# A Fourier-mixing and MLP kernel: the last chunk's output sent from SP and Scalar only, none from GpSimd

## Chip, cores, metric

The kernel runs on one core of a Trainium2 chip. The metric is the device time of one execution in microseconds (us), taken as the median of several.

## The reference

```python
batch, seq, dim = (8, 3008, 256);  d_ff = 2048

X = np.fft.fft(x, axis=1)
X = np.fft.fft(X, axis=2)
x = X.real.astype(np.float32).reshape(batch * seq, dim)

h = x @ w_in
g = h * np.clip(h + 3.0, 0.0, 6.0) / 6.0
out = g @ w_out                     # (24064, 256), float32
```

## The kernel before

The kernel works through four pairs of batches, twelve chunks to a pair. For each chunk TensorE computes both layers; the second layer's seven products are accumulated in PSUM, scaled by ScalarE, added up by GpSimd and transposed in 32 x 32 blocks by VectorE. SP sends the result to HBM. GpSimd also issues the loads: 16 pieces of the weights, 36 direct loads of `x` and 32 gathers.

The last chunk is different, since nothing follows to hide its end. VectorE does its additions (`finish_final`), and its two halves are sent by three engines in turn:

```python
def finish_final(ch):
    ...
    add(rn[:, 0, 0], e[:, 0], e[:, 1], nc.vector)
    turn(ch, os[0], 0, 0)
    ...
    turn(ch, os[0], 0, 1)
    send(ch, os[0], 0)                      # first half
    add_product(wn[:, 1], 4, wn[:, 0])
    for h in range(2):
        add(rn[:, 1, h], wn[:, 1], e[:, 2 + h], nc.vector)
        turn(ch, os[1], 1, h)               # the last transpose ends here
    send(ch, os[1], 1)                      # second half

def send(ch, o, m):
    queues = [nc.sync, nc.scalar, nc.gpsimd] if ch.final else [nc.sync]
    i = 0
    sl = 0
    while sl < ch.ns:
        b, k1 = ch.rows[m][sl]
        nb = 2 if sl + 1 < ch.ns and ch.rows[m][sl + 1] == (b + 1, k1) else 1
        for qd in range(DB):                # DB = 4
            queues[i % len(queues)].dma_start(
                out=out_k[ch.pr.p, k1, qd][:, 2 * b:2 * (b + nb)],
                in_=o[qd * DH:(qd + 1) * DH, 2 * sl:2 * (sl + nb)].rearrange(...))
            i += 1
        sl += nb
```

A half of the last chunk is eight sends, four of 32 KB and four of 16 KB. The loads that matter to the experiments are these:

```python
def load_forward(pr, c):
    ...
    nc.gpsimd.dma_start(out=xt[0:nr, 0:n, :], in_=rows[:, c * XC + 1:c * XC + 1 + n, :])
    if n < XC:
        nc.gpsimd.dma_start(out=xt[0:nr, n:XC, :], in_=rows[:, 0:1, :])
```

Of the kernel before, what the change touches and what calls it, by code (L numbers as in the profile page):

```python
# [56 lines left out]
def kernel(  # L57
# [10 lines left out]
    nc = tc.nc  # L68
# [338 lines left out]
    def finish_final(ch):  # L407
        n = ch.n
        e = ch.e[:, :, 0:n]
        w = epool.tile([P, 3, TB], F32, tag="w", bufs=1, name="w")  # L410
        ch.r = epool.tile([P, 2, 2, TB], F32, tag="r", name="r")
        wn, rn = w[:, :, 0:n], ch.r[:, :, :, 0:n]
        os = [epool.tile([P, TB // DH, 2, DH], F32, tag="o", name="o") for m in range(2)]

        def add_product(out, i, in1, sign=1.0):
            nc.vector.scalar_tensor_tensor(out, ch.acc[i // 2][:, i % 2, 0:n], sign / WS, in1,
                                           op0=AL.mult, op1=AL.add)

        add(rn[:, 0, 0], e[:, 0], e[:, 1], nc.vector)
        turn(ch, os[0], 0, 0)  # L420
        add_product(wn[:, 0], 5, e[:, 0], -1.0)
        add(wn[:, 2], wn[:, 0], e[:, 3], nc.vector)
        add_product(rn[:, 0, 1], 6, wn[:, 2])
        turn(ch, os[0], 0, 1)
        send(ch, os[0], 0)
# [3 lines that stand above are left out]
            turn(ch, os[1], 1, h)  # L429
        send(ch, os[1], 1)  # L430

    def store(ch, m):
        o = epool.tile([P, TB // DH, 2, DH], F32, tag="o", name="o")
        for h in range(2):
            turn(ch, o, m, h)
        send(ch, o, m)
# [4 lines left out]

    def send(ch, o, m):

        queues = [nc.sync, nc.scalar, nc.gpsimd] if ch.final else [nc.sync]
        i = 0
        sl = 0
        while sl < ch.ns:
            b, k1 = ch.rows[m][sl]
            nb = 2 if sl + 1 < ch.ns and ch.rows[m][sl + 1] == (b + 1, k1) else 1
            for qd in range(DB):  # L450
                queues[i % len(queues)].dma_start(
                    out=out_k[ch.pr.p, k1, qd][:, 2 * b:2 * (b + nb)],
                    in_=o[qd * DH:(qd + 1) * DH, 2 * sl:2 * (sl + nb)].rearrange("i j h e -> i j (h e)"),
                )
                i += 1
            sl += nb
# [383 lines left out]
```

## Time and profile before

| kernel before | |
|---|---|
| time, three runs | 2003.18, 2004.63, 2004.73 us |
| span of the profiled run | 2001.0 us |
| TensorE busy | 1965.6 us, 98% |
| last transpose starts | 1991.19 us |
| DMAs that GpSimd issues in the whole program | 88 (16 + 36 + 32 loads, 4 sends) |

The profile names engines PE (TensorE), DVE (VectorE), ACT (ScalarE), POOL (GpSimd) and SP; a trailing q (POOLq) marks an instruction of the sequencer, such as a send, a wait or a drain, which is not counted as busy. TensorE is idle for 35 us in all. Of these, 13 us lie in the first 100 us, before the work runs evenly, and 12.5 us after its last product; the other 10 us are spread over the 1900 us between. The change is in the end. The start of the last transpose is called T below.

### The profile page before, as it was taken

What the parts mean: (1) busy time and instruction counts of PE and PEld (TensorE: products, weight loads), DVE (VectorE), ACT (ScalarE), POOL (GpSimd) and SP (SyncE); (2) the same over time, 40 slices, a digit from 0 to 9 for tenths busy, and PEclk for the clock granted to TensorE, in tenths of its full rate; (3) what the DMA queues carried; (4) which work ended last, traced back from release to release, by engine and by line L of the source; (5) the groups of instructions that cost most, each with busy time, mean ns of one, the idle gap of its engine ahead of it and who ended that gap; (6) DMA issues with size and microseconds to landing.
All of it is one profiled execution on the core that took longest, in us unless ns stands there. A gap on an engine that the chain in (4) does not pass through costs nothing.

```text
span 2001.0 us, 28370 instructions
## 1 busy us (share of the span) xinstructions
PE 1965.6 (98%) x9178; PEld 1691.6 (85%) x9178; DVE 1440.1 (72%) x2711; ACT 700.3 (35%) x1196; POOL 1416.2 (71%) x1608
## 2 busy tenths in 40 slices
PE   8899999999999999999999999999999999999997
PEld 5588888888888888888888888888888888888886
DVE  5677767776777677776777767777678777777776
ACT  6533333333333333333333333333333333333322
POOL 3277778776777787777658877778666667667664
PEclk9899999999999999999999999999999999999999
DMA  9512212211111122110201221212110101101100
GB/s 296 143 28 58 51 40 50 57 36 35 29 34 51 41 52 59 47 51 25 50 17 30 70 57 39 51 44 52 35 27 20 27 17 26 33 12 27 27 12 19
DMA packets 158665, 93.54 MB, mean 47 GB/s; under 512 B 130635, under 2 KB 143467, under 8 KB 158518
## 3 DMA queue, kind: packets, MB, share of 16 engines
q1 hardware_dynamic: 148310, 57.99, 12.0%
q0 software_dynamic: 9600, 33.59, 6.0%
q8 instruction: 75, 1.23, 0.2%
q14 instruction: 72, 0.59, 0.1%
q10 hardware_dynamic: 608, 0.13, 0.0%
HBM read 54.32 MB, written 37.33 MB: 46 GB/s over the span
## 4 chain that ended last, share of the span: by engine, by line
PE 93%; DVE 3%; ACT 1%; issue 1%; POOL 0%; DVEq 0%; POOLq 0%; ACTq 0%
PE acc L382 55%; PE v L326 16%; PE u L326 16%; PE ps L280 2%; PE ps L226 2%; DVE a L358 1%; ACT t L355 0%; DVE u L339 0%; DVE s L331 0%; DVE o L440 0%; ACT PM L498 0%; PE wps L563 0%; DVE v L345 0%; DVE u L342 0%; ACT q L282 0%
## 5 line engine op out<-in xcount | busy, mean ns | idle before, releaser
L372 POOL TENSOR_TENSOR c<-a 128x512 f32<-128x512 f32 (+1 forms) x383 | 478.2, 1249 | 452.3 <-PE acc L382 358.3
L382 PE MATMUL acc<-c,G 128*128 128x256 f32 (+1 forms) x3072 | 712.0, 375 | 0.0
L355 ACT ACTIVATE t<-u,half 128x512 f32<-128x512 f32 (+2 forms) x416 | 272.5, 655 | 1105.7 <-DVE u L339 1094.1
L382 PEld LDWEIGHTS acc<-c,G 128*128 128x128 f32 x3072 | 577.5, 190 | 72.8
L331 DVE SCALAR_TENSOR_TENSOR s<-qn,WN,u 128x256 f32<-128x256 f32 x768 | 334.2, 476 | 352.8 <-PE u L326 352.4
L382 PE MATMUL acc<-a,G 128*128 128x256 f32 (+1 forms) x2304 | 551.7, 375 | 0.0
L382 PEld LDWEIGHTS acc<-a,G 128*128 128x128 f32 x2304 | 434.9, 190 | 57.7
L326 PE MATMUL v<-q,W 127*128 127x256 f32 x1536 | 398.6, 381 | 7.6 <-DVE a L358 7.6
L326 PE MATMUL u<-q,W 128*128 128x256 f32 x1536 | 395.4, 380 | 1.8 <-DVE a L358 1.5
L326 PEld LDWEIGHTS u<-q,W 128*128 128x128 f32 x1536 | 287.8, 190 | 59.7 <-issue 15.6
L326 PEld LDWEIGHTS v<-q,W 127*128 127x128 f32 x1536 | 290.2, 190 | 55.7 <-issue 8.2
L358 DVE SCALAR_TENSOR_TENSOR a<-t,u 128x512 f32<-128x512 f32 (+2 forms) x416 | 265.9, 646 | 96.0 <-ACT t L355 90.0
L372 POOL TENSOR_TENSOR c<-c,a 128x256 f32<-128x256 f32 (+1 forms) x383 | 274.7, 717 | 30.0
L372 POOL TENSOR_TENSOR c<-a,c 128x256 f32<-128x256 f32 (+1 forms) x383 | 274.5, 717 | 30.0
L339 DVE TENSOR_TENSOR u<-s,v 128x512 f32<-128x512 f32 (+1 forms) x384 | 263.1, 685 | 42.1 <-PE v L326 1.6
L355 ACT ACTIVATE t<-v,half 128x512 f32<-128x512 f32 (+1 forms) x384 | 257.1, 670 | 5.8 <-DVE v L345 4.4
L345 DVE TENSOR_TENSOR v<-v,s 128x512 f32<-128x512 f32 (+1 forms) x384 | 257.7, 671 | 1.1
L358 DVE SCALAR_TENSOR_TENSOR a<-t,v 128x512 f32<-128x512 f32 (+1 forms) x416 | 254.9, 619 | 0.5
L372 POOL TENSOR_TENSOR r<-w,e 128x256 f32<-128x256 f32 (+1 forms) x94 | 90.8, 987 | 3.7
L390 ACT ACTIVATE e<-acc 128x512 f32<-128x512 f32 (+2 forms) x190 | 86.3, 544 | 2.8 <-PE acc L382 2.7
L440 DVE STREAM_TRANSPOSE o<-r 128x256 f32<-128x256 f32 (+1 forms) x192 | 72.5, 415 | 0.4
L238 ACT COPY z<-ps 96x512 f32<-96x512 f32 x64 | 37.2, 581 | 82.8 <-PE ps L226 62.5
(91 smaller groups left out, 755.7 us busy)
## 6 DMA issues: line engine op xcount, KB each, us to landing
out_dram<-o SPq DMA_DIRECT2D x732, 32.0 KB
zd<-z SPq DMA_DIRECT2D x32, 384.0 KB
g<-zd SPq DMA_DIRECT2D x48, 256.0 KB
xt<-in_x_dram POOLq DMA_DIRECT2D x21, 384.0 KB, 4.0
qn<-qd SPq DMA_DIRECT2D x23, 256.0 KB
st<-in_moe_w_in_dram POOLq DMA_DIRECT2D x8, 512.0 KB, 11.1
st<-in_moe_w_out_dram POOLq DMA_DIRECT2D x8, 512.0 KB, 5.0
xt<-in_x_dram POOLq DMA_DIRECT2D x7, 376.0 KB, 3.9
```

Of the source, the lines that this page charges most:

```text
L226: nc.tensor.matmul(ps[0:PZ], F[0:PR, 0:PZ], y[:, 2 * i:2 * i + 2, :], start=True, stop=True)
L280: nc.tensor.matmul(ps[:, blk, 2 * u:2 * u + 2], g[:, kk, blk * (P + 1):blk * (P + 1) + P], T[:, :, gr, blk, kk], start=True, stop=True)
L326: nc.tensor.matmul(ps[:, i], W1[r, blk, f * P:(f + 1) * P], q[r, blk, of:of + KC], start=True, stop=True)
L331: nc.vector.scalar_tensor_tensor(s[:, i].rearrange("p k n -> p (k n)"), qn[:, of * N2:(of + KC) * N2], WN[:, f:f + 1], u[:, i].rearrange(" ...
L339: nc.vector.tensor_tensor(u[:, :, 0:ns], s[:, :, 0:ns], v[:, :, 0:ns], op=AL.add)
L345: nc.vector.tensor_tensor(v[:, :, 0:nm], v[:, :, 0:nm], s[:, :, 0:nm], op=AL.subtract)
L355: nc.scalar.activation(t, h, AF.Relu, bias=half[:], scale=scale)
L358: nc.vector.scalar_tensor_tensor(dst, t, 1.0, h, op0=AL.min, op1=AL.mult)
L372: (eng or nc.gpsimd).tensor_tensor(out, in0, in1, op=AL.add)
L382: nc.tensor.matmul(ch.acc[i // 2][:, i % 2, 0:ch.n], G[:, i, fc, :], mv, start=(fc == 0 and i % 2 == 0), stop=(fc == NF - 1), skip_group_c ...
L390: nc.scalar.mul(ch.e[:, k:i + 1, 0:ch.n], ch.acc[i // 2][:, 0:i + 1 - k, 0:ch.n], 1.0 / WS)
L440: nc.vector.transpose(o[:, 0:n // DH, h], ch.r[:, m, h, 0:n].rearrange("p (j i) -> p j i", i=DH))
```

## The change

The aim is to do without GpSimd's slower sends, and to let the two remaining queues share them evenly.

```diff
     def send(ch, o, m):
 
-        queues = [nc.sync, nc.scalar, nc.gpsimd] if ch.final else [nc.sync]
+        queues = [nc.sync, nc.scalar] if ch.final else [nc.sync]
         i = 0
```

## The prediction

> **What bounds the kernel now.** I read the engine table first, then the chain that ended last, then the end of the run piece by piece.
>
> The page's first part (engine, busy microseconds, share of the span, instructions) and, from the chain of waits over the last 26 us, its last pieces (start, length, what):
>
> ```profile
> PE 1965.6 (98%) x9178; PEld 1691.6 (85%) x9178; DVE 1440.1 (72%) x2711; ACT 700.3 (35%) x1196; POOL 1416.2 (71%) x1608
> ```
>
> ```profile
> 1991.19 0.39 DVE o L440
> 1991.58 0.29 issue
> 1991.87 0.56 POOL out_dram L451
> 1992.43 0.53 POOLq L835
> ```
>
> The reader is to see two things. TensorE holds the run for 98% of the span, and the change touches none of its instructions: the listing of the changed kernel's instructions shows the PE, DVE and compute ACT rows unchanged. So nothing before the last chunk's output can move by more than noise. And the chain ends at 1992.96 us while the span is 2001.0 us: 8.0 us at the end that the chain does not explain. The whole question lies there.
>
> Line 835 is the end of the program (the closing barrier). Asking for that line alone, in the whole span, gives (engine, operation, count, durations in ns as min/median/max, first and last start):
>
> ```profile
> L835 SPq EVENT_SEMAPHORE  x12: 17/28/28, 1993.9 to 2001.0; - x12
> L835 POOLq EVENT_SEMAPHORE  x4: 17/17/17, 2000.3 to 2000.9; - x4
> L835 POOLq DRAIN  x3: 46/103/7925, 1992.3 to 2000.7; - x3
> L835 SPq DRAIN  x3: 7/7/7, 1995.6 to 2000.5; - x3
> L835 ACTq DRAIN  x2: 8/82/156, 1993.0 to 2000.5; - x2
> ```
>
> The same line in the stretch 1995.4 to 1996.0 us:
>
> ```profile
> L835 SPq EVENT_SEMAPHORE  x3: 28/28/28, 1995.4 to 1995.5; - x3
> L835 SPq DRAIN  x2: 7/7/7, 1995.6 to 1995.7; - x2
> L835 POOLq DRAIN  x1: 7925/7925/7925, 1992.3 to 1992.3; - x1
> ```
>
> SP, which waits there for every DMA, is through at 1995.7 us. ACT's drain is over at 1993.1, DVE's at 1991.6, PE's at 1988.5. **One GpSimd DRAIN runs from 1992.30 for 7.925 us, to 2000.23 us.** Everybody waits for it; the barrier's own traffic then takes 0.78 us to 2001.0. The bound of the last stretch is therefore GpSimd's drain, and it holds the end 4.55 us longer (2000.23 less 1995.67) than the data do.
>
> Is the drain waiting for data? The DMA view for 1993.5 to 1994.0 shows the last packets, all queues ending by about 1993.8 (and 1994 to 1996 shows none):
>
> ```profile
> q0 software_dynamic: 32, 0.02, 13.8%
> q10 hardware_dynamic: 72, 0.01, 13.5%
> q1 hardware_dynamic: 23, 0.00, 4.0%
> ```
>
> and GpSimd's own four sends land quickly (the view of the output tensor, 1960 us to the end):
>
> ```profile
> L451 POOL DMA_DIRECT2D out_dram<-o x4: 545/565/618, 1990.2 to 1992.4; - x4
> DMA to landing us min/median/max: 2.0/2.1/2.2
> ```
>
> The last GpSimd send starts at 1992.42, so its data land near 1994.6, some 5.6 us before the drain ends. The drain is not a wait for data to arrive.
>
> **What the Trainium skill says.** "DMA: Bandwidth & Descriptors", section "Issuing engines are not separate DMA queues", says that several issuers share the same 16 DMA engines and that issuing from more of them saves only the sequencer's time. The trace agrees: all three queues' packets lie in the same stretch, and sends cost 0.43 us (SP), 0.44 us (ACT) and 0.55 to 0.62 us (GpSimd) of their issuer. By that page the third queue buys little. The same page's section on the anatomy of a DMA on the GpSimd path gives about 2.0 us of fixed cost; the 2.0 to 2.2 us above agree. "Perfetto Trace Analysis", section "Sequencer-only Instruction (DRAIN, etc)", says that a semaphore wait lies ahead of the profiled window; so these 7.9 us are the drain's execution, not a wait for the barrier. "VectorE: DVE Perf Modes", section "The DRAIN you can't avoid", tells of drains of some 12 ns, constant on all five engines, at a program's start and end. Here the trace disagrees: GpSimd's drains are 183 ns at the start, 7925, 103 and 46 ns at the end. No page explains the long one. It is the only drain that follows GpSimd sends directly.
>
> **The change part by part.**
>
> Removed: four GpSimd sends (two of 32 KB, two of 16 KB), 618 + 567 + 563 + 545 ns = 2.29 us of GpSimd. GpSimd's last work is then an addition that starts at 1982.66 and takes 0.59 us, so its drain begins near 1983. If that drain is now short, GpSimd is ready some 12 us before anybody else. Even if it keeps 7.9 us, it ends near 1991.2, before the last transpose (1991.57). In both cases it leaves the path: **4.55 us off the end.**
>
> Added: one more send of each size for SP and for ACT over the two halves: each half goes from 3 + 3 + 2 (SP, ACT, GpSimd) to 4 + 4. The page's spacing of SP's sends is 0.47 us (1991.96 to 1992.43). First half: SP starts at 1989.89, then 1990.25, 1990.72, and a fourth at about 1991.20, ending near 1991.64. Second half: its data are ready at 1991.57 and SP began it at 1991.60; now it can begin at 1991.68. But the semaphores of the hardware-queued sends go round over eight lanes, and the listing shows that the first send of the second half now waits for the landing of the first send of the first half (lane 2 on SP, 1 on ACT), which before was the second send's wait. That wait was already over at 1991.96 before, so it costs at most 0.3 us. I take 1991.8 for the start: sends at 1991.8, 1992.3, 1992.75, 1993.2. The last send from SP or ACT before began at 1992.44 and 1992.50, so **about 0.7 us later**.
>
> Packets: in 1989.5 to 1994.2 us the DMA view gives 736 packets for 16.2% of 16 engines over 4.7 us, or 16.5 ns each. GpSimd's 128 packets take 9.8%, 0.46 us of each engine. The same bytes by a hardware queue are 2 x 128 + 2 x 64 pieces of 256 B and 64 semaphore writes, 448 packets of 16.5 ns over 16 engines, 0.46 us too. The DMA work is the same.
>
> End: before, the last sends began at 1992.50 and SP had counted all of them at 1995.67, 3.2 us later, of which some 0.5 us is the row of waits that follows the last one that really held (SP's wait that started at 1995.19). Now 1993.2 + 3.2 = 1996.4 at the latest reckoning; the order of the waits may give back 0.2. I take SP done at 1996.3. The barrier adds 0.78: span 1997.1. Sum: 4.55 less about 0.65, **3.9 us saved**.
>
> **The rivals.**
> - The drain's 7.9 us is not tied to these sends, and starts late or ends on something at the end of the program (for example instruction fetches: one 8 KB fetch runs at 1996.1). For it: GpSimd's drain ends long after anything visible. Against it: every other engine's drain is under 0.5 us of its last work, or PE's 2.1 us, which merely covers queued matmuls. Then the end stays or is 0 to 1 us later: 2004 to 2005.5 us. I give this 10%.
> - The two hardware queues become the bound: the eight lanes are all taken by the first half, each second-half send waits for a landing, and landings stretch. Before, one of SP's sends (start 1991.96) was seen landed only 3.2 us later. For it: 16 sends share 8 lanes, where 12 did. Against it: the lane waits seen cost nothing. It would eat 1 to 2 us of the gain: 2001.5 to 2003.
> - The third queue was hidden anyway and the drain is all there is: up to 4.5 us saved, 2000.1 us.
>
> **Range and chances.** The three times before are 2003.18 to 2004.73 around 2004.63, and the profiled run took 2002.78, so one median is good to about 0.8 us. 2004.63 - 3.9 = 2000.7. With the second rival and the noise the range is 1999.2 to 2002.9; the first rival lies outside and takes most of the rest. 2% is 40 us, ten times the whole tail: within 2% is as good as certain.
>
> **What would show it.** In the changed profile: no software-queue packets after the last input; GpSimd's drain at line 835 starting near 1983 and over before 1992; SP's last drain before the barrier at about 1996.3; barrier traffic of some 0.75 us after that; the last send from SP starting near 1993.2. It is wrong if GpSimd's drain still ends last, if SP's wait for the landings ends after 1998, or if the span differs before 1989.

## More of the kernel before

All runs told of here were fast; no slow one enters a comparison. The ten experiments were compared with the kernel before on the same chip: the first four and the last two with runs of their own session (11 runs of the kernel before each), the other four with those same 11 runs of the first session and one new one.

## The result, and the profile after

The changed kernel took 1997.49 us (median of four runs, 1995.06 to 2001.73); the kernel before, in four runs, 2003.91. The ratio is 0.9971 with a 95% interval of 0.9953 to 0.9990: 2.0 to 9.4 us faster, so within 2%, as forecast. A ratio is the mean time of one kernel's fast runs over that of the other's fast runs, so it isn't quite the ratio of the medians. Five more rounds of the same kernel gave 1998.62 us and a ratio of 0.9970 (0.9957 to 0.9983). The predicted range was 1999.2 to 2002.9: the measured time lies below it.

The profiled execution took 2001.73 us, the slowest of the four, with a span of 2000.0 us. Compared by spans alone, the change would seem to be worth 1.0 us. The page's first part and the last pieces of the chain of waits show otherwise:

```profile
PE 1967.1 (98%) x9178; PEld 1692.0 (85%) x9178; DVE 1439.4 (72%) x2711; ACT 700.1 (35%) x1196; POOL 1413.5 (71%) x1604
```

```profile
1995.13 0.02 issue
1995.16 0.38 DVE o L440
```

The chain now ends with the last transpose, without GpSimd. That transpose starts at 1995.16 us, where it started at 1991.19 before: all of the run up to it is 4.0 us later. From there to the end of the span it is 1999.96 - 1995.16 = 4.80 us, and was 2001.01 - 1991.19 = 9.82 us. **The end gained 5.02 us, and the opening happened to lose 4.0.** The second layer's first group of products shows where the 4.0 us came from. Of each kernel, the view of the accumulators (durations in ns, then first and last start): before

```profile
L382 PE MATMUL acc<-a,G x2304: 324/379/634, 91.9 to 1986.8; 128*128 128x256 f32 x176, 128*128 128x192 f32 x16
```

and after

```profile
L382 PE MATMUL acc<-a,G x2304: 324/379/634, 96.7 to 1990.8; 128*128 128x256 f32 x176, 128*128 128x192 f32 x16
```

The second layer begins 4.8 us later, and its last product of this group starts 4.0 us later: the difference is there before the hundredth microsecond, in code that the change doesn't touch.

The end, by line 835, the closing barrier (count, durations in ns as min/median/max, first and last start):

```profile
L835 SPq EVENT_SEMAPHORE  x12: 17/28/28, 1997.5 to 1999.9; - x12
L835 POOLq EVENT_SEMAPHORE  x4: 17/17/17, 1999.2 to 1999.9; - x4
L835 POOLq DRAIN  x3: 51/103/7578, 1986.6 to 1999.7; - x3
L835 SPq DRAIN  x3: 7/7/7, 1999.1 to 1999.4; - x3
```

(A DRAIN here is an instruction that each engine executes before it reports to the barrier.) GpSimd's drain is still there and still takes 7.6 us, though GpSimd sent nothing of the output. But it starts at 1986.6, 8.6 us ahead of T, and is over 1 us ahead of T. SP, done at 1999.18, is now the last to come to the barrier, and GpSimd's first semaphore instruction there follows at once, at 1999.2. The last send of the program is one of ScalarE's, before and after:

```profile
L451 ACTq DMA_DIRECT2D out_dram<-o x6: 374/438/442, 1989.9 to 1992.5; - x6
```

```profile
L451 ACTq DMA_DIRECT2D out_dram<-o x8: 384/440/443, 1993.9 to 1997.2; - x8
```

In the kernel before, SP is done 3.2 us after that send's start (1995.67), in the changed kernel 2.0 us after it.

So two questions are left. What is this drain, if it doesn't belong to the sends? And why did the end gain 5.0 us where 3.9 were predicted?

### The profile page after: what moved, and what is told of

Same layout as the page of the kernel before. It is cut to its first block, busy times and chain, and to the rows that moved or that the text cites. A ratio compares the mean times of both kernels' runs of the same rounds, so it can differ in the third digit from the quotient of the medians.

```text
span 2000.0 us, 28370 instructions
## 1 busy us (share of the span) xinstructions
PE 1967.1 (98%) x9178; PEld 1692.0 (85%) x9178; DVE 1439.4 (72%) x2711; ACT 700.1 (35%) x1196; POOL 1413.5 (71%) x1604
## 4 chain that ended last, share of the span: by engine, by line
PE 92%; DVE 3%; ACT 1%; issue 1%; POOL 0%; DVEq 0%; ACTq 0%; POOLq 0%
PE acc L382 55%; PE v L326 16%; PE u L326 16%; PE ps L226 2%; PE ps L280 2%; DVE a L358 1%; ACT t L355 1%; DVE u L339 1%; DVE s L331 1%; DVE o L440 0%; ACT PM L498 0%; PE wps L563 0%; DVE v L345 0%; PE ps L223 0%; DVE u L342 0%
```

## The experiments

In the table, times are in us; "drain" is GpSimd's closing drain, "end" is the time from T to the end of the span; "SP done" is when SP has counted all landings (its drain ahead of the barrier); "n" is the number of DMAs that GpSimd issues in the program. All from one profile of each kernel; "changed, again" is a second profile of the same one.

| kernel | n | drain took | drain: start, end after T | SP done after T | end |
|---|---|---|---|---|---|
| before | 88 | 7.925 | 1.11, 9.04 | 4.48 | 9.82 |
| changed | 84 | 7.578 | -8.56, -0.98 | 4.02 | 4.80 |
| changed, again | 84 | 7.582 | -8.57, -0.98 | 4.04 | 4.83 |
| before, 40 tiny GpSimd copies more | 128 | 11.193 | 1.11, 12.30 | 4.51 | 13.09 |
| before, 27 loads moved to SP | 61 | 5.727 | 1.11, 6.84 | 3.96 | 7.63 |
| GpSimd in the first half only | 86 | 7.802 | -0.56, 7.24 | 3.67 | 8.02 |
| GpSimd in the second half only | 86 | 7.808 | 1.15, 8.96 | 4.40 | 9.74 |
| changed, 40 tiny GpSimd copies more | 124 | 10.845 | -8.56, 2.29 | 4.03 | 4.81 |
| SP alone | 84 | 7.578 | -8.56, -0.98 | 8.04 | 8.83 |
| changed, lanes shifted by one | 85 | 7.660 | -8.56, -0.90 | 3.78 | 4.56 |
| before, one early drain more | 88 | 2.557 | 1.11, 3.67 | 4.47 | 5.25 |
| before, 24 early drains more | 88 | 2.589 | 1.11, 3.70 | 4.50 | 5.59 |

Every kernel gave correct results.

### The changed kernel again

No edit. What was expected:

> The changed kernel once more, to see how much of the measured gain is the end of the run and how much is scatter of its opening. In the two profiles the changed kernel's opening (first 115 us) ran 4.0 us later than before's, and its end then took 5.0 us less, counted from the last transpose's start. Theory A (the drain): from the start of the last transpose to the end of the span before took 2001.01 - 1991.19 = 9.82 us, changed 1999.96 - 1995.16 = 4.80 us; here again 4.8 +- 0.2 us, and over five rounds the changed kernel is 5.0 us faster (ratio 0.9975). Rival: the opening differs with the kernel; then the gain over five rounds is far from 5 us (1 us, if the opening of the first profile is typical).

The end took 4.83 us, as in the first profile to 0.03 us. Over five rounds the ratio was 0.9970, some 6.0 us of 2002.73; its interval, 3.4 to 8.6 us, holds the 5.0 us of the end and excludes 1 us. The opening isn't slower with this kernel as such. Theory A (what was gained is the end) stands.

### Forty tiny copies more in the kernel before

```diff
+        if p == NP - 1:
+            junk = dpool.tile([40, NFC], F32, tag="junk", bufs=1, name="junk")
+            for j in range(40):
+                put(8 + 2 * j, lambda k: nc.gpsimd.dma_start(out=junk[k:k + 1, :], in_=WN[k:k + 1, :]), j)
```

> The kernel before with 40 tiny copies (64 bytes each, into a scratch tensor) issued by GpSimd during the last pair's steps, long before the end. GpSimd's drain at the program's end took 7925 ns in the kernel before, with 88 GpSimd-issued DMAs in the whole program, and 7578 ns in the changed one, with 84: 90.1 and 90.2 ns for each. Theory A: the drain costs about 90 ns for every DMA that GpSimd issued in the program. Then 128 x 90.1 = 11.5 us, the span ends 3.6 us later, ratio 1.0018. Rival B: the drain belongs to the last sends and is a fixed 7.6 to 7.9 us; then 7.9 us and the same time as before.

The closing barrier (here line 840) has

```profile
L840 POOLq DRAIN  x3: 46/103/11193, 1991.3 to 2003.0; - x3
```

The drain grew by 3.27 us, 82 ns for each copy, and the ratio was 1.0015 (1.0003 to 1.0027). The rival, a fixed drain that belongs to the last sends, falls. The figure of 90 ns was a little off: it supposed that the drain has no fixed part.

### The loads of later pairs issued by SP

```diff
-        nc.gpsimd.dma_start(out=xt[0:nr, 0:n, :], in_=rows[:, c * XC + 1:c * XC + 1 + n, :])
+        eng = nc.gpsimd if pr.p == 0 else nc.sync
+        eng.dma_start(out=xt[0:nr, 0:n, :], in_=rows[:, c * XC + 1:c * XC + 1 + n, :])
         if n < XC:
-            nc.gpsimd.dma_start(out=xt[0:nr, n:XC, :], in_=rows[:, 0:1, :])
+            eng.dma_start(out=xt[0:nr, n:XC, :], in_=rows[:, 0:1, :])
```

> The kernel before, where the direct loads of x for pairs 1 to 3 (27 DMAs) are issued by SP in place of GpSimd; the last chunk keeps its three queues. Theory A: 88 - 27 = 61 DMAs, so the drain takes 5.5 us, ends 2.4 us sooner, and the kernel is 2.4 us faster than before (ratio 0.9988) if the moved loads do no harm. Rival B: the drain stays at 7.9 us and the time the same.

The drain (line 836 here):

```profile
L836 POOLq DRAIN  x3: 46/103/5727, 1993.0 to 1999.3; - x3
```

It is 2.20 us shorter for 27 DMAs, 81 ns each; the end took 7.63 us, 2.19 less than before, and the ratio was 0.9983 (0.9971 to 0.9995). The moved loads were mostly of 376 or 384 KB each; the copies of the run before were of 64 bytes. **The drain's length goes by the count of GpSimd's DMAs, not by their size**: 0.71 us and 82 ns each gives all drains from 61 to 128 DMAs to within 0.1 us. These loads were issued more than 600 us before the end.

Most of the 0.71 us belongs to the instruction ahead. The drain's record begins while that one still runs: in the kernel before, GpSimd's last send ends 0.66 us into the drain, in the changed kernel its last addition ends 0.62 us into it. From that end on the drains last 7.26 us (88 DMAs), 6.95 (84), 10.53 (128) and 5.06 (61): 82 to 83 ns for each DMA, with next to no fixed part.

### GpSimd in the first half only, and in the second half only

```diff
-        queues = [nc.sync, nc.scalar, nc.gpsimd] if ch.final else [nc.sync]
+        queues = [nc.sync, nc.scalar] + ([nc.gpsimd] if m == 0 else []) if ch.final else [nc.sync]
```

The mirror has `m == 1`. Expected of the first:

> Three queues for the first half of the last chunk's output, SP and Scalar alone for the second. Theory A (the drain's start plus its length set the end): GpSimd's second and last send then starts some 1.7 us sooner, the drain takes 86 x 90.1 = 7.75 us and ends about 1.9 us sooner than before against the last transpose; from the last transpose's start to the end 7.9 us, 1.9 us faster than before and 3.1 slower than the changed kernel. Rival C (GpSimd's sends in the second half slow the landings, and that is what the end waits for): the end is as in the changed kernel, 4.8 us after the last transpose's start.

and of the second:

> SP and Scalar alone for the first half of the last chunk's output, all three queues for the second: the mirror of the run with GpSimd in the first half, with the same 86 GpSimd DMAs. The drains seen so far (5727 ns for 61 DMAs, 7578 for 84, 7802 for 86, 7925 for 88, 11193 for 128) lie near 0.71 us + 82 ns each. Theory A, so refined: the drain starts 1.1 us after the start of the last transpose as in the kernel before, takes 7.8 us and the span ends 9.7 us after that start (before 9.82), so this kernel is as slow as before and all of the gain hangs on when GpSimd's last send is. Rival: what counts is how many sends GpSimd has; then it lies half way, at 7.3 us, or with the first-half run at 7.97 us.

Their drains (first half, then second half):

```profile
L835 POOLq DRAIN  x3: 46/103/7802, 1991.5 to 1999.8; - x3
```

```profile
L835 POOLq DRAIN  x3: 46/103/7808, 1993.8 to 2002.1; - x3
```

Both have two GpSimd sends and drains of 7.80 and 7.81 us. In the first the drain starts 1.68 us sooner against T than before, and the end is 1.80 us shorter (ratio 0.9986, 0.9973 to 0.9999). In the second it starts as before, and the end is 9.74 us (ratio 0.9995, 0.9981 to 1.0010, not told from before). The place of GpSimd's last send decides, not the number of sends. Rival C, that the landings set the end of these kernels, falls too: SP is done 3.67 us after T in the first, and 3.6 us of waiting for the drain follow.

The pair also answers the second question. With GpSimd in the second half, SP's wait for landings shows

```profile
SPq L835 <- DMA out_dram<-o: 1.5, 1, 1.5
```

and the view of the output tensor gives GpSimd's sends 2.2 us from start to landing. The wait ends 3.45 us after T, when the GpSimd send that started at 1993.95 has landed (at 3.42), and SP is done at 4.40. Without GpSimd in the second half, SP is done at 3.67, though its own last send starts later (1.73 us after T against 1.44). With three queues at once the other two queues' sends land later too. By the semaphore updates in the traces, SP's and ScalarE's last sends take 2.18 and 2.25 us from start to landing with GpSimd in the second half, 1.80 and 1.95 in the kernel before, and 1.50 to 1.61 in the changed kernel and with GpSimd in the first half only. The 0.73 us between 4.40 and 3.67 are not this alone: the last landing is counted at 3.45 in the one and at 3.42 in the other, but in the first case the rest of SP's row of waits, with a pause of 0.375 us, still follows.

### Forty tiny copies more in the changed kernel

The edit is the one above, on the changed kernel.

> The changed kernel with the same 40 tiny GpSimd copies as in the run on the kernel before. Theory A: 124 DMAs make a drain of 10.9 us, but it starts 8.6 us before the last transpose's start and is over 2.3 us after it, before SP has counted the landings (4.0 us after it); so the span ends 4.8 us after that start, unchanged, ratio to before 0.9975. Rival: work that GpSimd left behind is paid for anyway; then 3.3 us later.

```profile
L840 POOLq DRAIN  x3: 46/103/10845, 1984.0 to 1997.1; - x3
```

The drain is 3.27 us longer, as it was in the kernel before, but it ends 2.29 us after T, ahead of SP, and the end is 4.81 us as without the copies. The ratio was 0.9981 (0.9967 to 0.9996), which holds the 0.9975 expected. The same 3.27 us that came straight off the end there are free here.

### SP alone

```diff
-        queues = [nc.sync, nc.scalar, nc.gpsimd] if ch.final else [nc.sync]
+        queues = [nc.sync]
```

> SP alone sends both halves of the last chunk (16 sends, spacing 0.475 us). Theory A says nothing here but that the drain is off the path; the issue term decides. The first half's 8 sends begin 1.30 us before the last transpose's start and end 2.5 us after it; the second half's last send starts 5.8 us after it, lands 1.5 us later, then 0.6 us of waits and 0.8 us of barrier: 8.7 us from the last transpose's start to the end, 3.9 us slower than the changed kernel, 1.1 us faster than before. Rival (sends are hidden behind the data's movement): no more than 1 us slower than the changed kernel.

The end took 8.83 us, 4.0 us more than with two queues. SP's sixteen sends (durations in ns, first and last start):

```profile
L451 SPq DMA_DIRECT2D out_dram<-o x16: 315/425/542, 1992.2 to 1999.4; - x16
```

The last starts 5.98 us after T, and its landing is counted 1.51 us later. The time of sixteen sends in a row isn't hidden. In time the ratio was 0.9993 (0.9978 to 1.0007), unclear against before, as 1.0 us less at the end would be. So the second queue is worth 4 us here.

### The semaphore lanes shifted by one

The sends from SP and ScalarE report their landings on eight semaphores in turn. Such a semaphore is called a lane here; SP waits for the lanes one after another at the end.

```diff
-            nc.sync.dma_start(out=pr.zq[:, :, :, c * XC + n].rearrange("b k c -> (b k c)"), in_=z[:, n, P])
+            (nc.gpsimd if pr.p == NP - 1 else nc.sync).dma_start(out=pr.zq[:, :, :, c * XC + n].rearrange("b k c -> (b k c)"), in_=z[:, n, P])
```

> The changed kernel with one tiny SP copy of the last pair issued by GpSimd, long before the end, so that every later SP and Scalar send takes the semaphore one lane earlier and SP's last send has the last lane in SP's closing row of waits, not the first. In the changed kernel the last landing waited for came 3.42 us after the last transpose's start, and ten further waits of 0.06 us followed it before SP's drain (4.02 us). Theory: these waits now lie before the landing; SP is done at about 3.55, and the span ends about 4.35 us after the last transpose's start, 0.45 us sooner than the changed kernel. Rival: the row of waits is SP's own pace (fetching the closing instructions) and ends as before, 4.8 us.

SP was done at 3.78 us after T, not 4.02, and the end took 4.56 us. That is 0.24 us, half of what was expected. The trace shows why: the expectation went by the landing of SP's last send, 3.41 us after T, but ScalarE's last send lands at 3.57. SP's wait for it is over at 3.59, and the two waits and two drains after it take 0.19 us. So the row of waits does follow the landings, as the theory has it, and the rival falls. In time (ratio 0.9976, 0.9962 to 0.9991) it can't be told from the changed kernel. It has the shortest end of all, by the profile alone.

### Draining earlier in the kernel before

These keep all three queues. One has

```diff
+        if p == NP - 1:
+            put(20, nc.gpsimd.drain)
```

and the other, beside each load of a later pair,

```diff
                 put(9 * c, load_x, nx, c)
+                put(9 * c + 1, nc.gpsimd.drain)
```

> The kernel before (three queues at the end) with one more GpSimd drain early in the last pair, after GpSimd's last load. So far the closing drain costs 0.71 us + 82 ns for each DMA that GpSimd issued in the whole program, whatever its size. Theory A1 (the drain settles what has been issued since the last drain): the early drain takes 0.7 + 84 x 0.082 = 7.6 us, the closing one 0.7 + 4 x 0.082 = 1.0 us; it is over 2.2 us after the last transpose's start, and the span then ends when SP is done (4.5) and the barrier with it: 5.3 us after that start instead of 9.8. GpSimd's stand-still of 7.6 us in the last pair may hold TensorE for up to 5 us, so the time may hardly move. Theory A2 (the closing drain's length is a count kept for the whole program): the closing drain stays 7.9 us, and the span ends 9.8 us after the last transpose's start.

> The kernel before (three queues at the end) with a GpSimd drain after each of the 24 loads of later pairs. Theory A1: the first of them takes about 4 us (some 37 DMAs of the opening), the others 0.9 us, beside TensorE's work where GpSimd has some slack; the closing drain takes 1.0 us, the span ends 5.3 us after the last transpose's start, so 4.5 us faster than before less what the drains hold up. Theory A2: closing drain 7.9 us, no gain, and the drains' time is lost on top where GpSimd has no slack.

With one early drain (the early one, line 752, and then the closing ones):

```profile
L752 POOLq DRAIN  x1: 7718/7718/7718, 1631.1 to 1631.1; - x1
```

```profile
L838 POOLq DRAIN  x3: 46/103/2557, 1998.3 to 2002.1; - x3
```

The early drain took the 7.7 us, and the closing one is 2.56 us, over 3.67 us after T. A1 is right, a drain settles what has been issued since the last; A2 falls. (1.0 us was expected of the closing one. It ends 0.22 us after GpSimd's last send has landed, and the next run shows that a drain waits for that.) The end took 5.25 us, from 9.82.

And GpSimd's pause cost TensorE nothing. In the timeline of GpSimd around the early drain, the additions go from 1631.13 us straight to 1638.97; yet TensorE's instructions before and after it are shifted by the same 5.97 us, to 0.01 us, against the kernel before. My fear of 5 us lost was wrong: GpSimd had that much lead there. By the time, this run is unclear: ratio 0.9992 (0.9975 to 1.0008). Its profile fell in an execution whose opening was 6.0 us later, and the four runs spread over 6.9 us.

With 24 early drains the first took 3.7 us, for the 35 DMAs of the opening, and the others 1.0 to 2.4:

```profile
L750 POOLq DRAIN  x24: 997/1770/3715, 93.9 to 1374.0; - x24
```

Each of the others has two or three DMAs to settle. The semaphore updates in the trace part them in two. Where the last of these DMAs landed early enough, the drain took 1.00 us for two and 1.09 for three (ten drains; during 0.76 us of it the addition ahead still ran). Where it landed later, the drain went on until then and ended 0.12 to 0.13 us after the landing (eleven drains of 1.7 to 2.4 us). Two drains of 1.8 us fit neither. **So a drain has two lower bounds, the count of DMAs and the landing of the last one**, and the closing drain here, too, ended 0.21 us after GpSimd's last landing.

The ratio was 0.9975 (0.9962 to 0.9987), so faster than before clear of noise, by 2.6 to 7.6 us. The end took 5.59 us. Of the 0.35 us more than with one drain, 0.30 lie in the barrier after GpSimd's last drain; what caused them was not traced. So the third queue can stay without its 4.5 us. It then does 0.4 us worse at the end than none: 5.25 against 4.80.

## Why the prediction was wrong

**That the end is held by GpSimd's drain, and that the change takes it off the path: right.** The drain began 8.56 us ahead of T and ended 0.98 us ahead of it; SP came last. "Near 1983" was its foreseen start, which is 8.2 us ahead of the T of the profile before. That "it is the only drain that follows GpSimd sends directly" pointed the wrong way, though: the drain stayed at 7.58 us without the sends. The prediction allowed for this case and it came out harmless, because an early start was enough. What it costs is settled by count: 82 ns for each DMA that GpSimd issued since its last drain, and 0.71 us that are mostly the instruction ahead.

**That the added sends cost 0.65 us: wrong, and this is the step that failed.** The prediction said: "Now 1993.2 + 3.2 = 1996.4 at the latest reckoning". The first number was good: SP's last send started 1.91 us after T, against the 2.0 foreseen. The second was mis-sized: from the start of the last send to SP being done it was 1999.18 - 1997.18 = 2.0 us, not 3.2. The 3.2 us were read from a kernel in which GpSimd's sends were also in the air. In that kernel SP waited until 1994.67 for GpSimd's last send, 2.25 us after it started, and then needed 1.0 us more for its row of waits. In the changed kernel the last landing it waited for is one of its own, counted 1.5 us after its start, and 0.6 us of waits follow. Of the 1.2 us too much, 0.8 is the landing and 0.4 the row of waits. The mirror runs agree on the landing: SP's and ScalarE's last sends take 2.2 us to land with GpSimd in the second half, 1.5 to 1.6 with GpSimd in the first half only. So the term was not -0.65 but +0.46 us (4.48 to 4.02), and the end gained 5.02 us in place of 3.9.

The 0.46 has two parts. SP's last send did start 0.66 us later after T, as foreseen, but the last landing that held SP was counted 0.06 us earlier (3.42 against 3.48). The other 0.40 is nearly all a pause of 0.375 us in SP's row of waits in the kernel before. The prediction took the wait after this pause, at 1995.19, for one that held, and said that SP's send of 1991.96 was "seen landed only 3.2 us later". That is a misreading: by the trace's semaphore updates this send had landed at 1993.60, 1.64 us after its start. In seven of the kernels, the one before among them, the pause stands ahead of the same instruction of SP's program, the 1232nd in the trace. In the changed kernel, with two sends more ahead of it, this instruction is the very one that waits for the last landing, and no pause is seen beside that wait. So this part of the gain is luck: it hangs on where the pause falls. What makes the pause stays open.

**That a median of three is good to 0.8 us: wrong too.** It was drawn from three runs that happened to agree. Single runs of the kernel before spread from 2000.19 to 2006.99 us in later rounds, with medians of 2002.72 (12 runs) and 2004.61 (11 runs). In the twelve profiles T lies between 1990.2 and 1997.2 us, and nearly all of that is there when the second layer starts, at 91.4 to 98.0 us. What scatters in the opening was not traced. Of the 7.1 us between the 2004.63 that the prediction started from and the 1997.49 measured, 5.0 are the end; the other 2.1 lie within this scatter. Put otherwise, of the 3.2 us by which the time fell below the 2000.7 foreseen, 1.1 belong to the step above and 2.1 to this one.

Had the first error alone been avoided, 2004.63 - 5.02 = 1999.6 would have been the prediction, inside its own range, but still 2 us above the median.

**The rivals.** That the drain ends on something else at the end of the program (10%) was wrong. That the eight lanes hold up the second half and cost 1 to 2 us was wrong: its first send started at 1995.70, 0.54 us after T where it was 0.41 before, and this 0.13 us went to the queue's own sends ahead of it. The 3.2 us named for this rival was the misreading told above. The third, that the queue was hidden and the drain is all (4.5 us), came nearest, and fell short of the 5.0 by the 0.46 told of above.

**The signs named.** GpSimd's drain over before the last transpose: seen. SP's last drain at about 1996.3, that is 5.1 us after T: it was 4.0. Barrier traffic of 0.75 us: 0.78. "If the span differs before 1989" was named as a sign of error, and it did differ by 4.0 us, from the scatter of the opening, which I hadn't thought of. For the same reason SP's wait ended after 1998, the other sign of error. No packets of GpSimd's queue after the last input: seen (none from 1400 us on).

## What to carry to other kernels

Ask what an engine leaves to its closing drain: one whose last piece of work is close to the end puts all of its drain behind it, while one that stops a few microseconds sooner, or drains once in the middle where it has a lead, gets it over for nothing, as here. When a send path is removed, don't carry over a start-to-landing time that was measured while that path was in use. And when an opening scatters by several microseconds, compare the end from a common instant in the trace, not by spans.

## What the Trainium skill lacked or had wrong

- "VectorE: DVE Perf Modes", section "The DRAIN you can't avoid", gives the drains at a program's start and end as some 12 ns, constant, on all five engines. GpSimd's closing drain took 5.7 to 11.2 us without an earlier drain, and 2.6 us with one.
- No page that I found says what a GpSimd drain costs after DMAs that GpSimd issued. "DMA: Bandwidth & Descriptors" splits a DMA of that path into a fixed and a variable part, and this third part is missing: 0.71 us (mostly the instruction ahead) and 82 ns for each DMA since the last drain, alike for 64 bytes and for 384 KB (61 to 128 DMAs, nine kernels and one repeat). None says either that the drain lasts until GpSimd's last DMA has landed, and 0.12 to 0.22 us more (eleven early drains and two closing ones).
- The same page, section "Issuing engines are not separate DMA queues", calls the issuers' time usually small relative to the DMA. For sixteen sends of 16 and 32 KB at the end it wasn't: one queue for two made the end 4.0 us longer, at 0.47 us a send, where the last one took 1.5 us from start to landing. I found no figure there for a send from SP or ScalarE from its start to its landing: the last ones took 1.50 to 1.61 us here with two queues, and up to 2.25 with three at once, where GpSimd's took 2.0 to 2.2.
